# Attention plus MLP on one core: when a slot's copy, its rounding rest, its low weights and its score items are issued

## Chip, cores, metric

One core of one Trainium2 chip. The metric is the device time of one execution in microseconds (us), lower is better; a comparison is made from several rounds in which both kernels run on the same chip. The engines are TensorE (PE, with its weight loads shown as PEld), VectorE (DVE), ScalarE (ACT), GpSimd (POOL) and SyncE (SP, which here only issues transfers). Each engine works through its own instructions in the order in which they were issued, and waits for the others through semaphores.

## What is computed

`x` has 2048 rows of 448 values. It is normalised (layer norm), and three things are added: `x` itself, an attention with 16 heads of 28 and one shared key/value head, and an MLP that normalises once more.

```python
xn = _layernorm(x)
q = (xn @ wq).reshape(B, S, 16, 28);  k = xn @ wk;  v = xn @ wv
p = softmax(einsum("bhqd,bkd->bhqk", q, k) * 28 ** -0.5)
attention = einsum("bhqk,bkd->bhqd", p, v).reshape(B, S, 448) @ wo
y = _layernorm(xn)
mlp = gelu(y @ w1 + b1, approximate=True) @ w2 + b2
out = x + attention + mlp            # w1: 448 x 1792, w2: 1792 x 448
```

## The kernel before, in words

Large products are made from rounded operands: a value is split into a high part in the type fp32r (a copy, "hh", "xh", "w2h") and a rest (value minus high part, rounded: "hl", "xl", "w2l"), and high*high, low*high and high*low are summed in PSUM.

There are three stages. First (to about 66 us) x is normalised and projected to q, k and v, and w1 is split. Second (to about 500 us) the MLP runs, with score work of the attention mixed in. Third the attention proper. The change touches the second stage.

The MLP stage is a row of slots, `slot(n)` at line 631. Slot n belongs to a chunk c of 512 rows and a block ft of 128 of the 1792 hidden columns; there are 4 x 14 = 56 of them, and two more that only drain. A slot holds:

- `mlp1` (line 583): 11 matmuls of 512 columns into the PSUM tile `ph` (one buffer). Then ACT makes `hx` (bias, L590) and `hz` (square, L591), and POOL two steps on `hz` (L592, L593). It hands back two functions for later: `middle` (L596 tanh on ACT, L597 and L598 on POOL) and `ending` (L603, the copy `hh` on ACT, and L605, the rounding rest `hl` on POOL).
- `mlp2` (line 609) for slot n - 2: 12 matmuls of 448 columns with `hh`, `hl` and the rows of w2. After the i-th of them it calls `stages[i]`. The table `stages` is made in `slot` (lines 643 to 646), and a second form of it stands for slots in `norms`.
- In chunk 0 every second slot (`split`, line 580) also splits two blocks of w2: `w2_split` (line 334) has ACT copy the high part (L337) and POOL make the low part (L338); then the next load of w2 is issued (`w2_load`).
- Five slots in each of chunks 0 to 2 (n = 5, 7, 9, 11, 13, then 19 to 27 and 33 to 41 in steps of two) run a step of the next chunk's normalisation, `norms[n]`: PE transposes into the same `ph` buffer, L271 on ACT, L272 on DVE, and the scaling of the next rows (L261 ACT, L262 DVE).

Between these matmuls a slot issues nine score items, spread evenly over its 23 matmuls (lines 681 to 689): the items stand behind matmuls 1, 4, 7, 9, 12, 14, 17, 19 and 22. An item is one matmul of 512 columns into a PSUM tile `m` of a pool with three buffers, and a DVE instruction that empties it. There are two kinds:

- A maximum item (`max_stream`, L508 and L509).
- A turned item (`turned_scores`, L542 and L543). Four of them fill one tile `raw` of 128 x 2048 values; `raw` has two buffers (`RAWS = 2`). After the fourth, two exponentials are queued. `turned_exp` (line 555, L560 on ACT) takes one from the queue each time that it is called; after the second, SP issues four stores of `raw` to DRAM (`td`, L563). The first L543 that writes the buffer again waits for these four stores.

In a slot that is not a `split` slot the first four items are turned items; all others are maximum items. `turned_exp` stands in `stages` twice, as `texp`.

Of the kernel before, what the change touches and what calls it, by code (L numbers as in the profile page):

```python
# [22 lines left out]
NF = F // P  # L23
# [15 lines left out]
def block_kernel(ctx, tc, x, wq, wk, wv, wo, w1, b1, w2, b2, out):  # L39
    nc = tc.nc  # L40
    pe, act, dve, pool = nc.tensor, nc.scalar, nc.vector, nc.gpsimd
    ctx.enter_context(tc.manual_schedule())

    def f(t):
        return t.bitcast(F32)
# [68 lines left out]
    def rawtile(shape):  # L114
        return tmp.tile(shape, F32, name="raw", bufs=2)
# [57 lines left out]
    def proj_steps(ps, wh, wl, xh, xl, cs=slice(0, CW)):  # L173
        n = 0
        ps = ps[:, cs]
        for b in range(3):
            for w, v in ((wh(b), xh[:, b, cs]), (wh(b), xl[:, b, cs]), (wl(b), xh[:, b, cs])):
                pe.matmul(ps, w, v, start=(n == 0), stop=False)  # L178
                n += 1
                yield  # L180
        pe.matmul(ps, wh(3), xh[:, 3, cs], start=False, stop=False)
        yield
        pe.matmul(ps, wh(3), xl[:, 3, cs], start=False, stop=True)
        yield
# [58 lines left out]
    def line(t):  # L243
        lines[t] = keep.tile([P, D], F32, name="a", bufs=4)
        nc.sync.dma_start(lines[t], xv[:, t, :])
# [83 lines left out]
    def w2_load(s):  # L329
        raw = rawtile([P, 2, D])  # L330
        nc.sync.dma_start(raw, w2[2 * s * P:(2 * s + 2) * P, :].rearrange("(b p) n -> p b n", p=P))
        wl_q.append(raw)

    def w2_split(s):
        raw = wl_q.pop(0)
        ab = slice(2 * s, 2 * s + 2)
        act.activation(w2h[:, ab, :], raw, AF.Copy)  # L337
        pool.tensor_sub(w2l[:, ab, :], raw, f(w2h[:, ab, :]))  # L338

    def q_slot(c, i):  # L340
        xh, xl = xts[c, False]
# [91 lines left out]
    for c in range(NCH):  # L433
        center, turn = norm_parts((c + 1) % NCH, c + 1 == NCH)
        for i in range(4):
# [7 lines left out]
            if i in ((2, 3) if c == 0 else (1, 3)):  # L443
                n = 2 * c + i // 3
# [21 lines left out]
    def load_q(u, blocks=range(4)):  # L466
        c, g = units[u]
        cols = slice(c * CW, (c + 1) * CW)
        if u < 2 and 0 in blocks:
            qst.append(xt_p.tile([P, 4, CW], F32R, name="xh"))  # L470
            pool.memset(f(qst[u]), 0.0)
        qs = qst[u % 2]
        for b in blocks:
            blk, i = ((1, 0), (2, 0), (0, 1), (3, 1))[b]
            nh = heads_of(u)
            src = qd[i][4 * DH * g:4 * DH * g + DH * nh, cols].rearrange("(j r) n -> r j n", r=DH)
            loads.dma_start(f(qs[32 * blk:32 * blk + DH, 0:nh, :]), src)
        qss[u] = qs
# [5 lines left out]
    def load_max(u):  # L484
        qs, mr = qss[u], mrs.pop(u)
        nh = heads_of(u)
        pm = mtile([nh * CT, P])
        pe.transpose(pm, mr[:, 0:nh * CT], ident)
        mn = keep.tile([4 * CT, 2, P], F32R, name="mn", bufs=1)[0:nh * CT]
        if u:  # L490
            act.activation(mn[:, 0, :], pm, AF.Copy, scale=-1.0)
        else:
            dve.tensor_scalar(mn[:, 0, :], pm, -1.0, 0.0, op0=ALU.mult, op1=ALU.add)
        dve.scalar_tensor_tensor(mn[:, 1, :], pm, -1.0, f(mn[:, 0, :]), op0=ALU.mult, op1=ALU.subtract)
        loads.dma_start(f(qs[60:61, 0:nh, :]), f(mn[:, 0, :]))
        loads.dma_start(f(qs[124:125, 0:nh, :]), f(mn[:, 1, :]))
# [78 lines left out]
    w2h = hp.tile([P, NF, D], F32R, name="w2h", bufs=1)  # L575
    w2l = hp.tile([P, NF, D], F32R, name="w2l", bufs=1)
# [3 lines left out]
    def split(c, ft):  # L580
        return c == 0 and ft % 2 == 1

    def mlp1(c, ft):
        yh, yl = xts[c, True]
        ph = php.tile([P, CW], F32, name="ph")
        fs = slice(ft * P, (ft + 1) * P)
        yield from proj_steps(ph, lambda b: w1h[:, b, fs], lambda b: w1l[:, b, fs], yh, yl)
        hx = hrp.tile([P, CW], F32, name="hx", bufs=2)
        hz = hrp.tile([P, CW], F32, name="hz", bufs=2)
        act.activation(hx, ph, AF.Identity, bias=b1t[:, ft:ft + 1])  # L590
        act.activation(hz, ph, AF.Square, bias=b1s[:, ft:ft + 1], scale=GELU[0] ** 0.5)  # L591
        pool.tensor_scalar(hz, hz, 1.0, 1.0, op0=ALU.mult, op1=ALU.add)  # L592
        pool.tensor_mul(hz, hz, hx)  # L593

        def middle():
            act.activation(hz, hz, AF.Tanh, scale=GELU[1])  # L596
            pool.tensor_scalar(hz, hz, 0.5, 0.5, op0=ALU.mult, op1=ALU.add)  # L597
            pool.tensor_mul(hx, hx, hz)  # L598

        def ending():  # L600
            hh = hrp.tile([P, CW], F32R, name="hh")
            hl = hrp.tile([P, CW], F32R, name="hl")
            act.activation(hh, hx, AF.Copy)  # L603
            hs[c, ft] = (hh, hl)
            pool.tensor_sub(hl, hx, f(hh))  # L605

        return middle, ending

    def mlp2(c, ft, stages):
        if ft == 0:  # L610
            m2s[c] = [m2p.tile([P, D], F32, name=f"m2_{k}") for k in range(CT)]
        m2 = m2s[c]
        hh, hl = hs.pop((c, ft))
        for k in range(CT):
            ts = slice(k * P, (k + 1) * P)
            pe.matmul(m2[k], hh[:, ts], w2h[:, ft, :], start=(ft == 0), stop=False)  # L616
            stages[3 * k]()
            yield
            pe.matmul(m2[k], hh[:, ts], w2l[:, ft, :], start=False, stop=False)  # L619
            stages[3 * k + 1]()  # L620
            yield
            pe.matmul(m2[k], hl[:, ts], w2h[:, ft, :], start=False, stop=(ft == NF - 1))  # L622
            if ft == NF - 1:
                t = CT * c + k
                a = lines.pop(t)
                dve.tensor_add(a, a, m2[k])
                nc.sync.dma_start(ad[:, t, :], a)
            stages[3 * k + 2]()
            yield

    def slot(n):
        nonlocal maxed
        if n < len(mslots) and split(*mslots[n]):
            blk = n // 2
            w2_split(blk)
            if blk + 2 < NF // 2:
                w2_load(blk + 2)
        middle = ending = none
        if n < len(mslots):
            middle, ending = yield from mlp1(*mslots[n])  # L640
        for _ in range(5 if n < 2 else 0):
            maxed += mxs.step()
        texp = turned_exp if n < len(mslots) - 1 else none
        stages = {1: texp, 2: texp, 5: middle, 9: ending}
        if n in norms:
            stages = {4: norms[n], 5: middle, 6: texp, 7: texp, 10: ending}
        if n >= 2:
            yield from mlp2(*mslots[n - 2], [stages.get(i, none) for i in range(12)])
        else:
            for i in sorted(stages):  # L650
                stages[i]()
# [1 line left out]
    def none():  # L653
        pass

    norms, maxed = {}, 0
    mslots = [(c, ft) for c in range(NCH) for ft in range(NF)]
    for c in range(1, NCH):
        g = norm_gen(c, lambda shape: php.tile(shape, F32, name="ph"))
# [4 lines left out]
    for n in range(len(mslots) + 2):  # L664
        c, ft = mslots[n] if n < len(mslots) else (NCH, n - len(mslots))
        if 3 <= ft < 11 and ft % 2 and c < NCH - 1:
            line(CT * (c + 1) + (ft - 3) // 2)
        if 9 < ft:
            line(CT * c + ft - 10)
            if ft > 10:  # L670
                a = lines[CT * c + ft - 11]
                pool.tensor_add(a, a, b2b)
        if ft == 0 and n:
            a = lines[CT * c - 1]
            pool.tensor_add(a, a, b2b)
        if (c, ft) == (NCH - 1, 8):
            load_q(0)
        if (c, ft) == (NCH - 1, 11):
            load_max(0)
        ts = 0  # L680
        for _ in slot(n):
            done += 1
            if n == len(mslots):
                maxed += mxs.step()
            elif n < len(mslots) and done * MLP_MAX // 46 > (done - 1) * MLP_MAX // 46:
                if ts < 4 and n < len(mslots) - 1 and not split(c, ft):
                    ts += tq.step()
                else:
                    maxed += mxs.step()
# [263 lines left out]
```

## Time and profile before

| what | value |
|---|---|
| median of 3 runs (lowest to highest) | 1139.19 us (1136.71 to 1139.23) |
| the profiled execution: its time | 1138.7 us |
| the profiled execution: its span, first to last instruction | 1136.9 us |
| granted TensorE clock over the span | 0.995 |

In the lists of the profile a row of the timeline gives the start in us, the duration in us, the engine, the line of the kernel, the operation, what it writes and reads, how many instructions are merged in the row, and in brackets the idle time of the engine just before and what ended it. A row of windows gives for each engine the busy time and the number of instructions, then the granted clock, the share of the DMA engines that was busy, and GB/s. "SPq" is SP issuing transfers. The tiles `ph` of the MLP show as `ph`, the w2 accumulators as `m<-w2h,hh` and the score items as `m<-ks,qm` (maximum) and `m<-ks,q` (turned).

### The profile page before, as it was taken

The numbers are of one execution on the slowest core, as the hardware profiler recorded it, in microseconds if no ns is written. First come the engines' busy times: TensorE is split into PE (matmuls) and PEld (weight loads), VectorE is DVE, ScalarE is ACT, GpSimd is POOL, SyncE is SP. The second block draws the span as 40 slices with busy tenths as digits, with TensorE's granted clock in tenths as the row PEclk, the third lists the DMA queues.
The fourth block names the chain that finished last, engine by engine and source line by source line (L and its number), as shares of the span: only waits on it lengthen the run. The fifth ranks groups of instructions, "written<-read, shape, count | busy, mean of one in ns | idle before, by whom it ended". The sixth has DMA issues, their size and how long they took to land.

```text
span 1136.9 us, 17010 instructions
## 1 busy us (share of the span) xinstructions
PE 1103.0 (97%) x5777; PEld 718.4 (63%) x5777; DVE 909.4 (80%) x1704; ACT 723.6 (64%) x953; POOL 564.4 (50%) x690
## 2 busy tenths in 40 slices
PE   9999899999999999999999999999999999999998
PEld 8777787877888888864544555554546444455444
DVE  7787787978888898895888887788886888866733
ACT  6765555666666666656766666467765666664673
POOL 6357787767776777772243425324432342342130
PEclk9999999999999999999999999999999999999999
DMA  8774445767776676866577797587786877975830
GB/s 273 207 226 128 123 109 129 189 172 188 195 191 169 172 204 167 206 179 152 135 176 162 175 230 197 123 206 190 161 195 164 188 169 186 225 162 124 198 85 33
DMA packets 113667, 195.11 MB, mean 172 GB/s; under 512 B 17070, under 2 KB 96100, under 8 KB 109740
## 3 DMA queue, kind: packets, MB, share of 16 engines
q1 hardware_dynamic: 100972, 172.34, 60.7%
q0 software_dynamic: 11200, 21.10, 7.4%
q8 instruction: 46, 0.75, 0.3%
q10 hardware_dynamic: 1408, 0.57, 0.2%
q14 instruction: 41, 0.34, 0.1%
HBM read 115.22 MB, written 77.71 MB: 170 GB/s over the span
## 4 chain that ended last, share of the span: by engine, by line
PE 71%; DVE 7%; DMA 6%; POOL 6%; ACT 5%; issue 2%; SPq 1%; ACTq 0%; DVEq 0%; POOLq 0%
PE po L820 19%; PE m L508 13%; PE s L867 12%; PE ph L178 6%; DVE mx L509 4%; PE m L542 4%; PE m L846 3%; PE m L622 2%; PE m L619 2%; PE m L616 2%; DMA td<-raw 2%; DMA qm<-qd 2%; POOL hx L598 1%; POOL hz L593 1%; PE qp L178 1%
## 5 line engine op out<-in xcount | busy, mean ns | idle before, releaser
L509 DVE TENSOR_REDUCE mx<-m 128x1 f32<-128x512 f32 x784 | 510.7, 685 | 97.1 <-PE m L508 85.9
L869 ACT ACTIVATE p<-s 128x1024 f32<-128x1024 f32 x326 | 315.6, 1027 | 163.0 <-PE s L867 161.6
L508 PE MATMUL m<-ks,qm 128*128 128x512 f32 x784 | 303.2, 411 | 3.0 <-DMA qm<-qd 1.9
L820 PE MATMUL po<-p,vs 128*32 128x512 f32 x2048 | 233.0, 595 | 0.0
L867 PE MATMUL s<-xh,ks 128*128 128x512 f32 x652 | 213.0, 412 | 2.7 <-ACT p L869 0.9
L508 PEld LDWEIGHTS m<-ks,qm 128*128 128x128 f32 x784 | 147.2, 189 | 89.7 <-DVE p L834 45.3
L543 DVE TENSOR_SCALAR_CACHE_REDUCE raw<-m 128x512 f32<-128x512 f32 x240 | 160.5, 689 | 31.6 <-PE m L542 12.9
L867 PEld LDWEIGHTS s<-xh,ks 128*128 128x128 f32 x652 | 114.2, 189 | 57.5 <-ACT p L869 37.2
L820 PEld LDWEIGHTS po<-p,vs 128*32 128x32 f32 x2048 | 60.0, 109 | 133.5 <-issue 132.9
L834 DVE STREAM_TRANSPOSE p<-half 128x1024 f32<-128x1024 f32 x120 | 141.6, 1218 | 3.1 <-PE po L820 3.1
L560 ACT ACTIVATE raw<-raw,m 128x1024 f32<-128x1024 f32 x120 | 133.2, 1151 | 0.0
L542 PE MATMUL m<-ks,q 128*128 128x512 f32 x240 | 97.1, 405 | 5.8 <-DVE raw L543 4.4
L603 ACT ACTIVATE hh<-hx 128x512 fp32r<-128x512 f32 x56 | 35.4, 632 | 97.5 <-POOL hx L598 97.1
L847 ACT ACTIVATE p<-m 128x512 f32<-128x512 f32 x132 | 79.0, 607 | 27.6 <-PE m L846 27.5
L605 POOL TENSOR_TENSOR hl<-hx,hh 128x512 fp32r<-128x512 f32 x56 | 72.4, 1293 | 41.6 <-ACT hh L603 41.6
L622 PE MATMUL m<-w2h,hl 128*128 128x448 f32 x224 | 83.6, 373 | 0.1
L619 PE MATMUL m<-w2l,hh 128*128 128x448 f32 x224 | 82.3, 367 | 0.0
L616 PE MATMUL m<-w2h,hh 128*128 128x448 f32 x224 | 82.0, 366 | 0.0
L593 POOL TENSOR_TENSOR hz<-hz,hx 128x512 f32<-128x512 f32 x56 | 72.5, 1296 | 4.7
L598 POOL TENSOR_TENSOR hx<-hx,hz 128x512 f32<-128x512 f32 x56 | 72.2, 1290 | 4.7
L768 POOL DMA_DIRECT2D tr<-ld x56 | 28.1, 508 | 87.6 <-DMA ld<-rc 87.6
L426 POOL DMA_DIRECT2D qm<-qd x108 | 55.2, 519 | 29.9 <-PE m L508 25.9
(167 smaller groups left out, 1504.8 us busy)
## 6 DMA issues: line engine op xcount, KB each, us to landing
td<-raw SPq DMA_DIRECT2D x240, 256.0 KB
half<-td SPq DMA_DIRECT2D x120, 512.0 KB
xh<-qd POOLq DMA_DIRECT2D x60, 168.0 KB, 7.6
a<-in_A_x_dram SPq DMA_DIRECT2D x32, 224.0 KB
qd<-qe SPq DMA_DIRECT2D x24, 256.0 KB
qm<-qd POOLq DMA_DIRECT2D x108, 56.0 KB, 6.8
qm<-qd SPq DMA_DIRECT2D x88, 56.0 KB
ad<-a SPq DMA_DIRECT2D x16, 224.0 KB
```

What stands on the lines that cost most here:

```text
L508: pe.matmul(pm, qm[:, t * P:(t + 1) * P], ks[:, n * CW:(n + 1) * CW], start=True, stop=True)
L509: dve.tensor_reduce(mx[:, CT * j + t, n:n + 1], pm, axis=AX.X, op=ALU.max)
L542: pe.matmul(sc, q3[i][:, t * P:(t + 1) * P], ks[:, n * CW:(n + 1) * CW], start=True, stop=True)
L543: dve.tensor_scalar(raw[:, :, 4 * n:4 * n + 4, :].rearrange("p r b i -> p b r i"), sc.rearrange("p (b r i) -> p b r i", r=4, i=32), SCALE, ...
L560: act.activation(raw[:, rs], raw[:, rs], AF.Exp, bias=m3[:, 4:5], scale=1.0)
L616: pe.matmul(m2[k], hh[:, ts], w2h[:, ft, :], start=(ft == 0), stop=False)
L619: pe.matmul(m2[k], hh[:, ts], w2l[:, ft, :], start=False, stop=False)
L622: pe.matmul(m2[k], hl[:, ts], w2h[:, ft, :], start=False, stop=(ft == NF - 1))
L820: pe.matmul(po[32 * j:32 * j + 32, :], vs[:, kt, :], ps.pop((u, kt, j)), start=(kt == 0), stop=(kt == NT - 1))
L834: dve.transpose(p.rearrange("p k (g j) -> p g k j", j=32), halves[u, kt // 8][:, :, 32 * (kt % 8):32 * (kt % 8) + 64].rearrange("p g (k j) ...
L867: pe.matmul(s[:, i], ks[:, (kt + k) * P:(kt + k + 1) * P], qss[u][:, j, :], start=True, stop=True)
L869: act.activation(p, s, AF.Exp, scale=SCALE)
```

## The change

Four things are done, all in the MLP stage.

1. `ending` (the copy `hh` on ACT and the rest `hl` on POOL) of slot n is no longer called in slot n but in slot n + 1, at `stages[0]`, where it stands behind that slot's L590 to L593 on ACT and POOL.
2. The low part of w2 is made by DVE, in a function `low` that is called at stage 2 (stage 3 in a `norms` slot); the next load of w2 is issued behind it.
3. The other entries of `stages` move: `texp` from 1 and 2 to 1 and 3; in a `norms` slot the normalisation from 4 to 5, `texp` from 6 and 7 to 6 and 8, `middle` from 5 to 7.
4. The turned items of a slot are its fifth to eighth item, not its first four. The call that queues their exponentials thereby stands behind the slot's last `texp`.

```diff
@@ w2_split
         act.activation(w2h[:, ab, :], raw, AF.Copy)
-        pool.tensor_sub(w2l[:, ab, :], raw, f(w2h[:, ab, :]))
+
+        def low():
+            dve.tensor_sub(w2l[:, ab, :], raw, f(w2h[:, ab, :]))
+            if s + 2 < NF // 2:
+                w2_load(s + 2)
+
+        return low
@@ slot
-        nonlocal maxed
-        if n < len(mslots) and split(*mslots[n]):
-            blk = n // 2
-            w2_split(blk)
-            if blk + 2 < NF // 2:
-                w2_load(blk + 2)
-        middle = ending = none
+        nonlocal maxed, ending
+        middle = low = none
+        closing, ending = ending, none
         if n < len(mslots):
+            if split(*mslots[n]):
+                low = w2_split(n // 2)
             middle, ending = yield from mlp1(*mslots[n])
...
-        stages = {1: texp, 2: texp, 5: middle, 9: ending}
+        stages = {0: closing, 1: texp, 2: low, 3: texp, 5: middle}
         if n in norms:
-            stages = {4: norms[n], 5: middle, 6: texp, 7: texp, 10: ending}
+            stages = {0: closing, 3: low, 5: norms[n], 6: texp, 7: middle, 8: texp}
...
-    norms, maxed = {}, 0
+    norms, maxed, ending = {}, 0, none
@@ the loop over slots
-        ts = 0
+        ts = items = 0
         for _ in slot(n):
...
-                if ts < 4 and n < len(mslots) - 1 and not split(c, ft):
+                items += 1
+                if items > 4 and ts < 4 and n < len(mslots) - 1 and not split(c, ft):
                     ts += tq.step()
                 else:
                     maxed += mxs.step()
```

Slot 0 has only four items, so its four turned items become maximum items, and four turned items move from the MLP stage to the attention stage (which issues what is left of both kinds).

## The prediction

> **What bounds the kernel now.** I read the page first, then windows by chunk, then the timeline of undisturbed slots, then the rows around the longest idle times of PE.
>
> ```profile
> span 1136.9 us, 17010 instructions
> PE 1103.0 (97%) x5777; PEld 718.4 (63%) x5777; DVE 909.4 (80%) x1704; ACT 723.6 (64%) x953; POOL 564.4 (50%) x690
> ```
>
> PE is busy for 97% of the span, so the change can win only where PE waits in the MLP stage, or lose by making it wait. How much there is to win shows in two windows, from L590 of slot 2 to L590 of slot 16 (slots 2 to 15: the rest of chunk 0 and two more), and from there to L590 of slot 55 (39 slots):
>
> ```profile
> core 0: us, PE busy (x) PEld busy (x) DVE busy (x) ACT busy (x) POOL busy (x), PEclk, DMA share, GB/s
> 85.47:197.84 112.37, 103.58 (x453) 84.99 (x452) 88.72 (x174) 60.71 (x87) 87.94 (x80) 0.97 0.47 121
> 197.84:488.50 290.66, 285.08 (x1287) 236.20 (x1286) 250.02 (x577) 189.41 (x252) 212.13 (x206) 1.00 0.72 186
> ```
>
> The yardstick is an undisturbed slot, here on ACT and on POOL:
>
> ```profile
> 415.59 0.69 ACT L590 ACTIVATE hx<-ph,b1t 128x512 f32<-128x512 f32 x1 [0.28 <-PE ph L183]
> 416.17 0.68 ACT L591 ACTIVATE hz<-ph,b1s 128x512 f32<-128x512 f32 x1
> 416.74 2.19 ACT L560 ACTIVATE raw<-raw,m 128x1024 f32<-128x1024 f32 x2
> 422.62 0.69 ACT L590 ACTIVATE hx<-ph,b1t 128x512 f32<-128x512 f32 x1 [0.28 <-PE ph L183]
> ```
> ```profile
> 416.94 0.62 POOL L592 TENSOR_SCALAR hz<-hz 128x512 f32<-128x512 f32 x1 [0.25 <-ACT hz L591]
> ...
> 422.42 1.30 POOL L605 TENSOR_TENSOR hl<-hx,hh 128x512 fp32r<-128x512 f32 x1 [0.74 <-ACT hh L603]
> ```
>
> A slot takes 422.62 - 415.59 = 7.03 us. POOL's chain in it, from L592 to the end of L605, takes 423.72 - 416.94 = 6.78 us: it just fits. Slots with a normalisation need more:
>
> ```profile
> L270 PE MATMUL ph<-ident,xn 128*128 128x128 f32 x48 | 8.3, 299 | 6.0 <-ACT hz L591 6.0
> ```
>
> These are 12 slots with four transposes each, 8.3 / 12 = 0.69 us a slot; four of them lie in the first window, eight in the second. So the first window is 112.37 - 14 x 7.03 - 4 x 0.69 = 11.2 us above undisturbed, the second 290.66 - 39 x 7.03 - 8 x 0.69 = 11.0 us.
>
> **Copy, rest and low part (edits 1 to 3).** In chunk 0 POOL also makes the low part of w2:
>
> ```profile
> 124.67 2.08 POOL L338 TENSOR_TENSOR w2l<-raw,w2h 128x896 fp32r<-128x896 f32 x1
> ```
>
> Every second slot has one, so POOL's chain there needs 6.78 + 2.08 / 2 = 7.82 us a slot against 7.03, and `ph`, which has one buffer, is emptied late. Taking L338 away, and filling POOL's waits by calling L605 a slot later behind L593, cuts the chain to its bare work, well below 7.03. `hl` is needed only by `mlp2` two slots on; issued behind L593 of the next slot it ends some 3.5 us behind that slot's L591, over 2 us before the slot after reaches the matmul that reads it. So the 11.2 us can go. What is paid for it is the low part on DVE:
>
> ```profile
> L803 DVE TENSOR_TENSOR otl<-oc,oth x2: 426/426/427, 1129.1 to 1131.6; 128x256 fp32r<-128x256 f32 x2
> L272 DVE TENSOR_TENSOR xl<-ph,xh x12: 691/692/692, 127.2 to 387.9; 128x512 fp32r<-128x512 f32 x12
> ```
>
> From 0.426 us for 256 columns and 0.692 for 512 follow 1.09 for 896 (estimate); bounds are 0.692 and POOL's 2.08 for the same work. Six of them in the first window raise DVE from 88.72 to 95.3 us, below the 101.2 that the window would then last, so DVE isn't the bound. But `low` stands in DVE's queue in front of L272, on which the next slot's first matmul waits through `ph`, and in front of score items that free `m`. I take 2 us for that (bounds 0, and 6 for twice the duration). Net for chunk 0: -9.2 us.
>
> **The turned items (edit 4).** This is the part that decides. `raw` has two buffers; a buffer filled in slot n is filled again in slot n + 2 and must be stored by then. Before, all fits:
>
> ```profile
> 412.62 0.69 DVE L543 TENSOR_SCALAR_CACHE_REDUCE raw<-m 128x512 f32<-128x512 f32 x1
> ...
> 426.70 0.69 DVE L543 TENSOR_SCALAR_CACHE_REDUCE raw<-m 128x512 f32<-128x512 f32 x1
> ```
>
> The buffer filled from 412.62 is exponentiated by 416.74 + 2.19 = 418.93 and written again at 426.70, 7.77 us later. What the stores need shows where DVE did wait for them; the exponentials of that buffer, SP's issue of four stores in another slot, and DVE's end of the wait:
>
> ```profile
> 343.73 2.18 ACT L560 ACTIVATE raw<-raw,m 128x1024 f32<-128x1024 f32 x2
> ```
> ```profile
> 418.96 3.25 SPq L563 DMA_DIRECT2D td<-raw  x4
> ```
> ```profile
> 352.70 0.69 DVE L543 TENSOR_SCALAR_CACHE_REDUCE raw<-m 128x512 f32<-128x512 f32 x1 [1.08 <-DMA td<-raw]
> ```
>
> From 345.91 to 352.70 are 6.79 us, of which the issue alone is 3.25. So 7.77 left a slack of 1 us.
>
> After the change the fourth turned item of a slot stands behind its 19th matmul, and the last `texp` of that slot behind the 15th: in the changed program's order on ACT each pair of exponentials stands in the next slot, behind `hh`. Counted from L590 of that slot (h): the exponentials ended at h + 3.34 before (418.93 - 415.59); `hh` in front of them adds 0.63 less the 0.1 by which neighbours on ACT overlap (L590 starts 0.58 ahead of L591 and lasts 0.69), so they end at h + 3.87, and the stores land at h + 10.66. The buffer is wanted again by the fifth item of the slot after. That item's place is seen before too:
>
> ```profile
> 133.24 0.40 PE L508 MATMUL m<-ks,qm 128*128 128x512 f32 x1
> ```
> ```profile
> 133.30 0.69 ACT L590 ACTIVATE hx<-ph,b1t 128x512 f32<-128x512 f32 x1 [1.20 <-PE ph L183]
> ```
> ```profile
> 121.60 0.40 PE L508 MATMUL m<-ks,qm 128*128 128x512 f32 x1
> ```
> ```profile
> 122.04 1.33 DVE L509 TENSOR_REDUCE mx<-m 128x1 f32<-128x512 f32 x2 [0.20 <-PE m L508]
> ```
>
> Its matmul starts 0.06 us before L590, and DVE begins 0.44 after a matmul's start: h + 7.03 + 0.38 = h + 7.41. The stores are 3.25 us late, in every slot from 16 on (in chunk 0 only every second slot has turned items, so a buffer rests twice as long there). Behind DVE's waiting L543 stand all score items; `m` has three buffers, so PE stops at the eighth item. The restart:
>
> ```profile
> 464.27 0.69 DVE L543 TENSOR_SCALAR_CACHE_REDUCE raw<-m 128x512 f32<-128x512 f32 x1 [2.46 <-DMA td<-raw]
> ```
> ```profile
> 465.03 0.50 PE L542 MATMUL m<-ks,q 128*128 128x512 f32 x1 [0.98 <-DVE raw L543]
> ...
> 417.65 0.40 PE L508 MATMUL m<-ks,qm 128*128 128x512 f32 x1
> ```
>
> PE goes on 0.76 us after DVE, and from the eighth item (417.65) to the next L590 (422.62) are 4.97, with 0.1 for the slow first matmul 5.07. So L590 of slot n + 2 can't come before that of slot n plus 3.87 + 6.79 + 0.76 + 5.07 = 16.49 us: two slots take 16.49, not 14.06. Loss 2.43 a pair.
>
> In a normalisation slot the exponentials come later:
>
> ```profile
> 354.63 0.69 ACT L590 ACTIVATE hx<-ph,b1t 128x512 f32<-128x512 f32 x1 [0.27 <-PE ph L183]
> ...
> 356.65 0.60 ACT L271 ACTIVATE xh<-ph 128x512 fp32r<-128x512 f32 x1 [0.75 <-PE ph L270]
> ...
> 358.55 2.18 ACT L560 ACTIVATE raw<-raw,m 128x1024 f32<-128x1024 f32 x2
> ```
>
> They end at h + 6.10. `hh` fills the 0.75 in front of L271, and L596 stands among them as before, so I keep 6.10: 6.10 + 6.79 + 0.76 + 5.07 = 18.72 against 14.06 + 0.69. Loss 3.97 a pair; the last of each five does no L261 and loses some 0.7 less. Slots 16 to 54 are 39, of which ten pairs hold a normalisation: 9.5 x 2.43 + 8 x 3.97 + 2 x 3.3 = 61.5 us.
>
> On top comes the clock. PE's start at the eighth item is late by 3.25 + 0.38 + 0.76 - 2.06 = 2.3 us in a plain pair (417.65 is h + 2.06), idle 2.2 since a matmul's 0.40 overlaps the next; in a normalisation pair, where two L590 lie 7.03 + 0.69 = 7.72 apart, by 6.10 + 6.79 - 7.72 + 0.76 - 2.06 = 3.9. What such gaps did:
>
> ```profile
> 125.41 0.48 PE L270 MATMUL ph<-ident,xn 128*128 128x128 f32 x1 [2.37 <-ACT hz L591]
> ...
> 175.50 0.33 PE L270 MATMUL ph<-ident,xn 128*128 128x128 f32 x1 [2.57 <-ACT hz L591]
> ...
> 531.63 0.76 PE L508 MATMUL m<-ks,qm 128*128 128x512 f32 x1 [1.87 <-DMA qm<-qd]
> ...
> 248.85 0.50 PE L542 MATMUL m<-ks,q 128*128 128x512 f32 x1 [1.25 <-DVE raw L543]
> ```
> ```profile
> 125.40:128.80 3.40, 3.39 (x11) 3.03 (x12) 1.60 (x3) 1.31 (x3) 3.22 (x3) 0.50 0.62 172
> 176.60:180.00 3.40, 3.40 (x10) 2.91 (x10) 2.58 (x4) 0.27 (x2) 3.21 (x3) 0.50 0.24 68
> 531.60:535.00 3.40, 3.37 (x8) 2.72 (x9) 1.98 (x3) 1.50 (x3) 0.09 (x1) 0.50 0.03 5
> 248.80:252.20 3.40, 3.35 (x17) 2.72 (x18) 3.18 (x9) 1.54 (x3) 1.51 (x3) 1.00 0.95 234
> ```
>
> All three of 1.87 us and more were followed by 3.4 us at a granted clock of 0.50; the one of 1.25 was not. Half a clock for 3.4 us costs 1.7, and as it falls on the tail of the slot and the first matmuls of the next, it lies on the loop. I take it in all 19.5 pairs, 33.2 us (bounds 0 and 33.2). The Trainium skill (page "TensorE: Matmul & The Clock Gate", Part 1, "What's actually happening") says otherwise: the clock falls to half only after at least one idle window of about 3.4 us. By that rule the plain pairs would keep the clock (second rival); the three gaps above disagree with it.
>
> The four turned items that move to the attention stage cost nothing there: DVE's two kinds last the same, and their two exponentials fall on ACT, which PE covers.
>
> Sum: 1136.9 - 9.2 - 11.0 (the old disturbances of slots 16 to 54, which the loop replaces) + 61.5 + 33.2 = 1211.4 of span. The profiled execution took 1138.7, 1.8 more than its span, and the median is 1139.2: 1213 us.
>
> **Rivals.**
> - The clock falls only in the long stalls, of 3.9 us: 10 x 1.7 in place of 33.2, 1197 us. For it: the rows hold only three cases near 2.2. The skill's page named above would give this.
> - It never falls, since the two slots of a pair share the wait (1.2 each, like the gap of 1.25): 1180 us. Against it: the first wait falls whole into one slot, and nothing evens it out.
> - Not slower: the stores land in time. The point from which it decides is 7.41 - 3.87 = 3.54 us after the exponentials. Then only edits 1 to 3 count: 1136.9 - 9.2 - 11.0 + 1.8 = 1118 us. For it: where DVE didn't wait, the landing isn't seen. Against it: SP needs 3.25 us to issue the four, which leaves the last 0.3.
> - SP is held up by other loads, as for the buffer written again at 464.27, whose exponentials ended at 454.10:
>
> ```profile
> 451.91 2.19 ACT L560 ACTIVATE raw<-raw,m 128x1024 f32<-128x1024 f32 x2
> ```
>
> That took 10.17 us, 3.4 more than 6.79; in four of the pairs, 1226 us.
>
> **From these to the numbers.** Forecast 0.5, long stalls only 0.2, no fall 0.18, SP held up 0.06, not slower 0.06 (nearly all of it faster). 0.3% is about what a measurement of this kernel tells from no change, and no case but the last comes near. Range 1176 to 1228: it reaches from the case without a fall to SP held up, and leaves out the last and the blur of the bounds. Faster 0.05, same 0.01, slower 0.94.
>
> **What would show it.** DVE's idle time in front of L543 ended by the stores of `raw` is the largest wait of the MLP stage, some 80 us (9.5 x 3.25 + 10 x 4.8). Before:
>
> ```profile
> DVE raw L543 <- DMA td<-raw: 12.4, 10, 2.5
> ```
>
> L590 of slots 2 to 16 spans about 103 us, of slots 16 to 55 about 374, with long and short slots in turn and stretches at a clock of 0.50. POOL's wait of L605 for L603 is gone. If DVE hardly waits for the stores, my edit 4 is wrong; if it waits but slots 16 to 55 take about 341, the clock is; if slots 2 to 16 don't get shorter, POOL wasn't the bound of chunk 0.

## The result, and the profile after

| | median of the runs | ratio to before, 95% interval |
|---|---|---|
| before | 1139.21 us (1136.71 to 1141.84) | |
| after | 1210.18 us (1205.29 to 1216.39) | 1.0626 (1.0585 to 1.0668) |

The change makes the kernel 6.3% slower; 1213 us were forecast. The profiled execution of the changed kernel is its shortest, 1205.29 us. In the changed kernel every line from L338 on has a higher number: L590 (`hx`) is now L596, L543 (turned item) L549, L560 (exponentials) L566, L563 (stores) L569, L605 (rest) L611, and DVE's low part is L340.

The head of the page of the profile:

```profile
span 1203.5 us, 17023 instructions
...
PE 1117.9 (93%) x5777; PEld 725.2 (60%) x5777; DVE 917.2 (76%) x1711; ACT 713.8 (59%) x953; POOL 550.8 (46%) x683
```

PE works 15 us longer than before (slots 16 to 54 hold ten stretches of 3.41 us at half clock), the span is 66.6 us longer, and so PE's share falls from 97% to 93%. The same two windows as before, from L596 of slot 2 to that of slot 16, and on to that of slot 55 (columns: PE, PEld, DVE, ACT, POOL busy, granted clock, DMA share, GB/s):

```profile
83.74:188.99 105.25, 101.98 (x466) 84.91 (x465) 98.09 (x187) 57.99 (x84) 79.21 (x75) 1.00 0.46 122
188.99:550.28 361.29, 303.51 (x1283) 245.18 (x1282) 249.14 (x578) 180.78 (x250) 209.65 (x207) 0.95 0.60 150
```

Before, they took 112.37 and 290.66. So the 66.6 us of span are: -1.7 ahead of slot 2 (85.47 to 83.74), -7.1 in slots 2 to 15, +70.6 in slots 16 to 54, and +4.8 behind (the rest of the span is 653.2, it was 648.4). The stretch of +70.6 seen closer, over two slots without a normalisation (rows of the timeline, most left out):

```profile
481.93 0.69 ACT L596 ACTIVATE hx<-ph,b1t 128x512 f32<-128x512 f32 x1 [5.00 <-PE ph L183]
...
483.60 2.19 ACT L566 ACTIVATE raw<-raw,m 128x1024 f32<-128x1024 f32 x2
...
485.81 3.25 SPq L569 DMA_DIRECT2D td<-raw  x4
...
489.02 0.69 ACT L596 ACTIVATE hx<-ph,b1t 128x512 f32<-128x512 f32 x1 [2.71 <-PE ph L183]
...
492.68 0.69 DVE L549 TENSOR_SCALAR_CACHE_REDUCE raw<-m 128x512 f32<-128x512 f32 x1 [3.48 <-DMA td<-raw]
...
493.44 0.50 PE L548 MATMUL m<-ks,q 128*128 128x512 f32 x1 [2.19 <-DVE raw L549]
...
498.53 0.69 ACT L596 ACTIVATE hx<-ph,b1t 128x512 f32<-128x512 f32 x1 [5.13 <-PE ph L183]
```

The reader sees the predicted chain. The exponentials end at 485.79, which is h + 3.86 (483.60 + 2.19 - 481.93). SP issues four stores at once. 6.89 us after the exponentials DVE may write the buffer, at 492.68, after an idle time of 3.48; PE goes on 0.76 later, having stood for 2.19. The slots take 7.09 and 9.51 us in turn, 16.60 a pair; forecast were 16.49. The waits of the changed kernel:

```profile
DVE raw L549 <- DMA td<-raw: 55.6, 20, 5.3
...
PE m L548 <- DVE raw L549: 50.3, 25, 4.0
```

The wait for the stores is 55.6 us (it was 12.4). POOL's wait of L605 for L603, 41.6 us before, is in the list no more.

### The profile page after: what moved, and what is told of

The parts are those of the page before. It is cut to its first block, busy times and chain, and to the rows that moved or that the text cites. A ratio compares the mean times of both kernels' runs of the same rounds, so it can differ in the third digit from the quotient of the medians.

```text
span 1203.5 us, 17023 instructions
## 1 busy us (share of the span) xinstructions
PE 1117.9 (93%) x5777; PEld 725.2 (60%) x5777; DVE 917.2 (76%) x1711; ACT 713.8 (59%) x953; POOL 550.8 (46%) x683
## 4 chain that ended last, share of the span: by engine, by line
PE 66%; DMA 11%; DVE 9%; ACT 7%; SPq 3%; issue 3%; POOL 1%; ACTq 0%; DVEq 0%; POOLq 0%
PE po L825 18%; PE m L514 13%; PE s L872 11%; DMA td<-raw 7%; PE ph L178 6%; DVE mx L515 4%; ACT raw L566 3%; PE m L548 3%; PE m L851 3%; DMA qm<-qd 3%; SPq L569 2%; PE m L628 2%; PE m L622 2%; PE m L625 2%; PE m L736 1%
## 5 line engine op out<-in xcount | busy, mean ns | idle before, releaser
L514 PE MATMUL m<-ks,qm 128*128 128x512 f32 x784 | 311.1, 419 | 17.6 <-DVE raw L549 7.1
L549 DVE TENSOR_SCALAR_CACHE_REDUCE raw<-m 128x512 f32<-128x512 f32 x240 | 156.5, 688 | 91.4 <-DMA td<-raw 55.6
L514 PEld LDWEIGHTS m<-ks,qm 128*128 128x128 f32 x784 | 150.1, 192 | 117.6 <-DVE p L839 45.3
L596 ACT ACTIVATE hx<-ph,b1t 128x512 f32<-128x512 f32 x56 | 38.6, 690 | 217.6 <-PE ph L183 215.2
L548 PE MATMUL m<-ks,q 128*128 128x512 f32 x240 | 100.9, 420 | 50.7 <-DVE raw L549 50.3
L566 ACT ACTIVATE raw<-raw,m 128x1024 f32<-128x1024 f32 x120 | 134.8, 1151 | 0.0
L598 POOL TENSOR_SCALAR hz<-hz 128x512 f32<-128x512 f32 x56 | 35.2, 628 | 173.0 <-ACT hz L597 172.9
L548 PEld LDWEIGHTS m<-ks,q 128*128 128x128 f32 x240 | 45.4, 189 | 71.6 <-DVE raw L549 60.5
L599 POOL TENSOR_TENSOR hz<-hz,hx 128x512 f32<-128x512 f32 x56 | 75.5, 1348 | 4.7
```

What stands on the lines that cost most here:

```text
L514: pe.matmul(pm, qm[:, t * P:(t + 1) * P], ks[:, n * CW:(n + 1) * CW], start=True, stop=True)
L548: pe.matmul(sc, q3[i][:, t * P:(t + 1) * P], ks[:, n * CW:(n + 1) * CW], start=True, stop=True)
L549: dve.tensor_scalar(raw[:, :, 4 * n:4 * n + 4, :].rearrange("p r b i -> p b r i"), sc.rearrange("p (b r i) -> p b r i", r=4, i=32), SCALE, ...
L566: act.activation(raw[:, rs], raw[:, rs], AF.Exp, bias=m3[:, 4:5], scale=1.0)
```

## Experiments

In the expectations, theory A is the prediction's: the two buffers of `raw` are filled again before their stores have landed. B says that the loss comes from the copy and rest that are issued late, or from the low part in DVE's queue. C says that DVE's L262 (the scaling of 64 columns in a normalisation), which is held up while POOL works, is behind it. All ratios are to the kernel before.

### Edits 1 to 3 without edit 4

```diff
-                if items > 4 and ts < 4 and n < len(mslots) - 1 and not split(c, ft):
+                if ts < 4 and n < len(mslots) - 1 and not split(c, ft):
```

> Edits 1 to 3 alone: the turned items are a slot's first four again, so their exponentials run in the same slot. Theory A (the two buffers of raw: refilled before their stores land): the wait for the stores falls back to some 12 us or less, and what is left is the shorter POOL chain: L590 of slots 2 to 16 spans about 105 us as in the changed kernel, of slots 16 to 55 about 285 to 292; time 1128 us (1120 to 1136). The exponentials end 0.53 us later than before (behind the copy), which leaves 0.45 of the 1 us of slack. Theory B (the loss comes from the copy and the rest being late, or from the low part in DVE's queue, which backs up the three buffers of m): still about 1200 us.

Measured: 1130.31 us (1127.48 to 1133.72), ratio 0.9929 (0.9907 to 0.995). Its windows by slots 2, 16 and 55:

```profile
84.28:188.96 104.68, 101.82 (x466) 85.07 (x465) 98.13 (x186) 59.56 (x86) 79.22 (x75) 1.00 0.51 133
188.96:476.93 287.97, 280.64 (x1283) 236.29 (x1282) 255.96 (x577) 180.88 (x250) 210.26 (x207) 1.00 0.74 187
```

The gain in chunk 0 is all there (104.68), and slots 16 to 54 are as quick as before. The whole loss hangs on edit 4.

### Edit 4 alone

The kernel before, with the turned items as a slot's fifth to eighth item:

```diff
-                if ts < 4 and n < len(mslots) - 1 and not split(c, ft):
+                items += 1
+                if items > 4 and ts < 4 and n < len(mslots) - 1 and not split(c, ft):
```

> The kernel before with edit 4 alone: only the turned items move to places five to eight. Theory A: the exponentials run in the next slot and end at h + 3.34 (no copy in front of them), so the stores are 2.72 us late and a plain pair of slots takes 15.96 us, a normalisation pair as long as in the changed kernel; with half of the pairs losing 1.7 us to the clock, 1195 us (1180 to 1212), and chunk 0 is as long as before (112 us). Theory B: 1139 us, within 10.

Measured: 1220.7 us (1218.88 to 1222.26), ratio 1.0721 (1.0699 to 1.0743): slower still than the changed kernel. B is refuted, since copy, rest and low part are where they were. A has the direction, but the time lies above its range (1180 to 1212). The second window, and the wait:

```profile
197.20:566.73 369.53, 306.40 (x1280) 248.91 (x1279) 243.42 (x577) 189.55 (x251) 212.95 (x208) 0.94 0.58 148
```
```profile
DVE raw L543 <- DMA td<-raw: 78.1, 21, 6.2
```

Slots 16 to 54 take 369.5, which is 89.8 above an undisturbed 279.7 (39 x 7.03 + 8 x 0.69). The clock fell 13 times in them, 22 us at 1.7 each, and slot 55 to the end takes 653.3 in place of 648.4, for which the expectation had nothing. The rest of the miss stays open.

### The exponentials in their own slot

The changed kernel, with `texp` behind the slot's eighth item:

```diff
-        stages = {0: closing, 1: texp, 2: low, 3: texp, 5: middle}
+        stages = {0: closing, 2: low, 5: middle, 8: texp, 10: texp}
...
-            stages = {0: closing, 3: low, 5: norms[n], 6: texp, 7: middle, 8: texp}
+            stages = {0: closing, 3: low, 5: norms[n], 7: middle, 8: texp, 10: texp}
```

> The changed kernel, with both exponentials called at stages 8 and 10 of their own slot, behind the call that queues them; the turned items stay the fifth to eighth. Theory A: the exponentials end at about h + 6.3, the stores land at h + 13.1, and the buffer is wanted at h + 14.44: no wait, no fall of the clock, 1120 us (1112 to 1130). If instead late turned items are bad in themselves (theory B, or less room on DVE in the second half of a slot): about 1200 us as in the changed kernel.

Measured: 1130.9 us (1126.43 to 1134.63), ratio 0.993 (0.9904 to 0.9956). The items stay as edit 4 puts them; only the exponentials, and so the stores, start earlier. The wait for the stores is gone:

```profile
DVE raw L549 <- DMA td<-raw: 0.8, 1, 0.8
```

That takes 79 us off edit 4's price: the loss is the time from the last turned item of a fill to the landing of its stores, not the place of the items. But the run is some 10 us over the expected 1120, just outside its range. In slots 16 to 54 most slots without a normalisation take 7.03 us, the longest 7.63; six with one take 8.85 to 8.90. One of these (unfiltered timeline):

```profile
227.80 1.34 DVE L262 TENSOR_SCALAR xn<-a,lnq,lnqb 128x64 f32<-128x64 f32 x1
227.81 1.29 POOL L611 TENSOR_TENSOR hl<-hx,hh 128x512 fp32r<-128x512 f32 x1
...
229.06 0.68 DVE L549 TENSOR_SCALAR_CACHE_REDUCE raw<-m 128x512 f32<-128x512 f32 x1
...
229.81 0.50 PE L514 MATMUL m<-ks,qm 128*128 128x512 f32 x1 [1.13 <-DVE raw L549]
```

L262 works on 64 columns and lasts 1.34 us, until POOL's L611 ends; behind it the turned items are late, and PE stands for 1.13. The same line in the kernel before and in the changed one, all its runs in the MLP stage (min/median/max in ns):

```profile
L262 DVE TENSOR_SCALAR xn<-a,lnq,lnqb x12: 304/352/948, 107.7 to 372.9; 128x64 f32<-128x64 f32 x12
```
```profile
L262 DVE TENSOR_SCALAR xn<-a,lnq,lnqb x12: 657/1311/1382, 107.7 to 412.9; 128x64 f32<-128x64 f32 x12
```

Moving L611 into the next slot (edit 1) put it beside L262. This was not foreseen.

### The low part back on POOL

Edits 1 and 3, with the low part on POOL; it stays at edit 2's later place in the slot, and so does the next load of w2:

```diff
-            dve.tensor_sub(w2l[:, ab, :], raw, f(w2h[:, ab, :]))
+            pool.tensor_sub(w2l[:, ab, :], raw, f(w2h[:, ab, :]))
```

> Edit 1 with its spacing of the stages, but the low part of w2 back on POOL (called at stage 2 or 3) and the turned items first. Theory A: POOL's bare work is 5.1 us a slot, with half of 2.08 on top 6.2, below 7.03, so chunk 0 is as short as with the low part on DVE (105 us for slots 2 to 16): 1126 us (1118 to 1136). Rival: it was the low part on DVE that relieved chunk 0, and without it slots 2 to 16 span 112 us again: 1137 us.

Measured: 1128.83 us (1127.1 to 1131.01), ratio 0.9917 (0.9899 to 0.9935), the first window 105.60. So chunk 0 is relieved without DVE: beside edit 1, by which POOL no longer waits for `hh` (a wait of 41.6 us before), the move of the low part to DVE adds 0.9 us in this window and nothing in the time. That L605's later call does it, and not the low part's later place on POOL, is argued: no run has edit 1 with the low part at its old place.

### The stores on two queues

The changed kernel, with two of the four stores issued by ACT:

```diff
-                nc.sync.dma_start(td[u][:, :, 4 * t + a, :],
+                (nc.scalar if a % 2 else nc.sync).dma_start(td[u][:, :, 4 * t + a, :],
```

> The changed kernel with two of the four stores of raw issued by ACT, two by SP; nothing else. Theory A (the loop through raw's stores sets the pace): the issue of four takes SP 3.25 us, of two 1.6, so the stores land some 1.6 us earlier; a plain pair loses 0.8 us in place of 2.43, a normalisation pair some 2.4 in place of 3.97, and only the latter can still lose the clock: L590 of slots 16 to 55 spans 310 to 325 us (361 in the changed kernel), time 1150 to 1180 us. If the landing hangs on the transfer and not on the issue, or the loop isn't the cause: 1205 us or more.

Measured: 1218.25 us (1211.32 to 1223.77), ratio 1.0691 (1.0655 to 1.0728): not A's 1150 to 1180; the expectation's other branch came, 1205 or more "if the landing hangs on the transfer and not on the issue". One fill in the timeline, and the window of its transfer:

```profile
201.55 2.19 ACT L566 ACTIVATE raw<-raw,m 128x1024 f32<-128x1024 f32 x2
...
203.76 1.21 SPq L569 DMA_DIRECT2D td<-raw  x2
203.77 1.85 ACTq L569 DMA_DIRECT2D td<-raw  x2
...
210.34 0.69 DVE L549 TENSOR_SCALAR_CACHE_REDUCE raw<-m 128x512 f32<-128x512 f32 x1 [3.25 <-DMA td<-raw]
```
```profile
204.80:209.90 5.10, 4.33 (x20) 3.38 (x18) 2.06 (x3) 3.38 (x5) 3.35 (x4) 1.00 0.86 206
```
The same in the changed kernel, for the fill ahead of the one shown first:

```profile
474.23 2.18 ACT L566 ACTIVATE raw<-raw,m 128x1024 f32<-128x1024 f32 x2
...
483.18 0.69 DVE L549 TENSOR_SCALAR_CACHE_REDUCE raw<-m 128x512 f32<-128x512 f32 x1 [1.07 <-DMA td<-raw]
```
```profile
477.60:482.70 5.10, 5.10 (x24) 4.31 (x23) 4.35 (x10) 0.77 (x2) 1.41 (x2) 1.00 0.86 206
```

All four are issued within 1.9 us and not 3.25, yet DVE goes on 6.60 us after the exponentials (210.34 - 203.74); in the changed kernel it was 6.77 (483.18 - 476.41). In both kernels the 1 MB moves in about 5.1 us at 206 GB/s with the DMA engines busy for 0.86. Over all fills of slots 15 to 53 for which DVE stood more than 0.5 us, the time from the exponentials' end to DVE's start is 6.77 to 9.27 with a median of 7.0 in the changed kernel, and 6.60 to 9.72 with a median of 7.1 with two queues. So issuing faster did not make the stores land earlier; that the transfer sets the landing is read from these windows. This kernel is even 8 us slower than the changed one: slots 16 to 54 take 365.9 us (361.3), with half-clock stretches of 41.0 us in all (34.1), and the part behind slot 55 takes 657.7 (653.2). Why the latter is longer stays open.

### Edit 2 alone, at two places

The kernel before, with the low part on DVE. In the first run it stands where POOL's stood, at the start of the slot:

```diff
-        pool.tensor_sub(w2l[:, ab, :], raw, f(w2h[:, ab, :]))
+        dve.tensor_sub(w2l[:, ab, :], raw, f(w2h[:, ab, :]))
```

> The kernel before with edit 2 alone: the low part of w2 on DVE, at its old place at the slot's start. POOL's chain falls from 7.82 to 6.78 us a slot in chunk 0, just below 7.03. If POOL's load is what bounds chunk 0: slots 2 to 16 span about 106 us (112 before), 1132 us (1127 to 1137). If it is the place of the copy and the rest in the queues that counts, 111 us or more and 1138.

Measured: 1163.38 us (1162.39 to 1165.86), ratio 1.0214 (1.02 to 1.0229): neither number of the expectation. The first window takes 134.3 us in place of 112.4, and the timeline shows why:

```profile
94.12 0.63 ACT L603 ACTIVATE hh<-hx 128x512 fp32r<-128x512 f32 x1 [2.11 <-POOL hx L598]
94.66 0.93 ACT L337 ACTIVATE w2h<-raw 128x896 fp32r<-128x896 f32 x1
...
95.62 1.42 DVE L338 TENSOR_TENSOR w2l<-raw,w2h 128x896 fp32r<-128x896 f32 x1 [3.59 <-ACT w2h L337]
96.97 3.07 DVE L509 TENSOR_REDUCE mx<-m 128x1 f32<-128x512 f32 x5
...
97.70 0.50 PE L508 MATMUL m<-ks,qm 128*128 128x512 f32 x1 [3.44 <-DVE mx L509]
```

ACT makes `hh` first, which waits for POOL, then the high part of w2; DVE's low part waits for that, and all score items of the slot wait behind it on DVE. If this is the cause, the same work at a later place costs nothing, which the second run tries (the next load of w2 behind it, as in the change):

```diff
-        stages = {1: texp, 2: texp, 5: middle, 9: ending}
+        stages = {1: texp, 2: texp, 3: low, 5: middle, 9: ending}
```

> The kernel before, and the low part of w2 on DVE as in the run at 1163, but issued behind the third step of mlp2 (stage 3), with the next load of w2 behind it; copy and rest stay where they were before. If the loss of that run came from the place in DVE's queue (low at the head of the slot, waiting for ACT's high part, which stands behind the copy hh and so behind POOL, with all score items of the slot behind it), this one loses none of it: ACT's high part is long done when DVE comes to low, PE's waits of 3.4 us for L509 are gone, slots 2 to 16 take 104 to 109 us and the kernel 1128 to 1134. If it came from the work of 1.1 to 1.4 us on DVE itself, it stays near 1160.

Measured: 1133.93 us (1131.75 to 1135.37), ratio 0.9956 (0.9939 to 0.9972), the first window 106.51. The place was worth 29 us, the work itself hides (the next load of w2 moved with it, but in neither run does ACT's copy of w2 wait for a load):

```profile
94.83 1.20 DVE L340 TENSOR_TENSOR w2l<-raw,w2h 128x896 fp32r<-128x896 f32 x1
```

It starts without a wait. So edit 2 does relieve chunk 0 (112.4 to 106.5) where edit 1 isn't there; either suffices. That both remove the same excess on POOL fits, but is argued.

### L262 on ACT

In the kernel of edits 1 and 3:

```diff
-            dve.tensor_scalar(xn[:, D:512], src[:, 384:448], scale[:, t:t + 1], bias[:, t:t + 1],
-                              op0=ALU.mult, op1=ALU.add)
+            if second and c:
+                act.activation(xn[:, D:512], src[:, 384:448], AF.Identity, bias=bias[:, t:t + 1], scale=scale[:, t:t + 1])
+            else:
+                dve.tensor_scalar(xn[:, D:512], src[:, 384:448], scale[:, t:t + 1], bias[:, t:t + 1],
+                                  op0=ALU.mult, op1=ALU.add)
```

> The fourth kernel of the first four (edit 1 with its spacing, low part on POOL, turned items first), and the 64 columns of L262 are scaled by ACT in the MLP stage, not by DVE. Theory C: in a normalisation slot DVE's L262 lasts 1.35 us in place of 0.30 since it waits for POOL's instruction (the rest is issued there now), and PE loses 1.1 us at the next slot's start; without it slots 16 to 55 span about 281 us in place of 288 and slots 2 to 16 some 2 less: 1120 us (1115 to 1125). If the 1.1 us come from the wait for ACT's L271 instead: 1129 us.

Measured: 1119.24 us (1117.2 to 1121.26), ratio 0.9825 (0.9809 to 0.9842). On ACT the step lasts 0.43 us, and nothing waits for it. The first window takes 101.79, against 101.2 undisturbed.

The same edit with the turned items at 5 to 8 and the exponentials in their own slot (low part on POOL):

> As the one before, but with turned items as the fifth to eighth and both exponentials at stages 8 and 10 of their own slot. Theory A and C together: no wait for the stores in any slot, 280 us for slots 16 to 55, within 3 us of the one before (1117 to 1123). If late turned items had a cost of their own, it shows here as more than 3 us.

Measured: 1118.63 us (1115.58 to 1127.35), ratio 0.9835 (0.9807 to 0.9863). These two are the quickest found, and can't be told apart. Windows of the second:

```profile
82.45:185.58 103.13, 101.80 (x466) 84.81 (x465) 88.95 (x177) 61.49 (x91) 90.11 (x83) 1.00 0.51 133
185.58:466.15 280.57, 280.11 (x1283) 236.00 (x1282) 246.22 (x570) 188.69 (x258) 210.27 (x207) 1.00 0.75 191
```

Slots 16 to 54 take 280.6, with 279.7 undisturbed: edit 4 itself costs nothing once its stores start early enough and L262 is off DVE.

The same edit in the changed kernel as it is:

> The changed kernel, and the 64 columns of L262 scaled by ACT instead of DVE in the normalisations of chunks 1 to 3. In the kernels with edits 1 and 3 that step alone was worth about 9.6 us (1128.8 to 1119.2), where the next slot stood 1.13 us on DVE. A: in the changed kernel the two buffers of raw set the loop, and a normalisation slot of that kernel gains only where DVE's turned items, not the stores, end last: between 3 us (the four normalisation slots of chunk 0) and 10 us less than its 1210, so 1200 to 1207, with the wait for the stores still over 50 us. C: if the conflict of L262 with POOL were the main cause of the loss and the wait for the stores its consequence, 1150 or less.

Measured: 1205.53 us (1202.99 to 1209.04), ratio 1.0589 (1.0568 to 1.061). C is refuted as the cause of the loss. The second window, and the wait:

```profile
186.97:554.65 367.68, 306.74 (x1283) 249.82 (x1282) 241.68 (x570) 183.61 (x259) 210.04 (x207) 0.94 0.58 147
```
```profile
DVE raw L552 <- DMA td<-raw: 84.4, 24, 5.8
```

With L262 out of the way the same loop stands on the stores all the more, 84.4 us.

## Why the prediction was right, point by point

**What bounds, and which edit decides.** Right: undoing edit 4 takes 80 us away, edit 4 alone brings 82 (1220.7 - 1139), and starting the stores earlier removes all of it (1130.9 against 1130.31).

**Chunk 0.** A gain of 9.2 was forecast; 1.7 + 7.1 = 8.8 came. But the 2 us that I charged for the low part in DVE's queue were charged to the wrong instruction. Low part on DVE or on POOL makes the first window 104.68 or 105.60; taking L262 off DVE takes it from 105.60 to 101.79. The duration of 1.09 us was right only where no POOL instruction was under way when L340 began (1.08, once in these rows of the changed kernel, min/median/max in ns); the other six began while one was, and lasted longer:

```profile
L340 DVE TENSOR_TENSOR w2l<-raw,w2h x7: 1081/1284/2177, 79.8 to 168.0; 128x896 fp32r<-128x896 f32 x7
```

**The loop through `raw`.** Slots 16 to 54 take 361.3 us, 81.6 above undisturbed. The clock fell ten times in them; at the prediction's 1.7 us each that is 17.0, and 64.6 remain for the loop. 61.5 were forecast. Its links agree one by one: exponentials at h + 3.86 (3.87), landing 6.89 later (6.79; over all fills the median is 7.0), PE 0.76 behind DVE, a plain pair of 16.60 (16.49). A normalisation pair agrees too: from L596 of slot 37 (389.27) to that of slot 39 (409.63) are 20.36 us, with one fall of the clock in it, so 18.7 without (18.72). Only its exponentials come sooner than forecast, at h + 5.03 to 5.91 in the ten normalisation slots, not 6.10. The wait of 55.6 us is below the "some 80": here other releasers are named for part of DVE's idle time (91.4 us in all ahead of L549), and with L262 gone it is 84.4.

**The clock: the term that was mis-sized.** 33.2 us were forecast, a fall in each of 19.5 pairs; 17.0 came. The profiled span lies 7.9 below the sum (1203.5 against 1211.4: +3.1 loop, -16.2 clock, +0.4 in and ahead of chunk 0, +4.8 attention). The rule I took from three gaps, that 1.87 us of idle time are enough and 1.25 are not, lacks a condition. Three stalls of the changed kernel, by windows of 3.41 us (busy PE is the third number, the granted clock the third from the end):

```profile
339.19:342.60 3.41, 1.47 (x7) 0.96 (x6) 0.43 (x1) 3.41 (x5) 2.72 (x3) 1.00 0.73 199
342.60:346.01 3.41, 3.08 (x8) 2.62 (x9) 2.95 (x10) 0.21 (x1) 2.26 (x3) 0.50 0.70 157
438.18:441.59 3.41, 1.69 (x9) 1.16 (x7) 0.00 (x0) 3.41 (x6) 2.51 (x3) 1.00 0.90 222
441.59:445.00 3.41, 1.93 (x9) 1.69 (x10) 2.65 (x10) 0.43 (x1) 2.49 (x3) 1.00 0.68 161
445.00:448.42 3.42, 3.42 (x17) 2.83 (x16) 3.21 (x6) 0.27 (x1) 0.00 (x0) 1.00 0.81 200
506.45:509.86 3.41, 1.35 (x7) 0.89 (x5) 0.38 (x1) 3.41 (x5) 3.23 (x4) 1.00 0.77 192
509.86:513.27 3.41, 3.04 (x8) 2.58 (x9) 2.97 (x10) 0.10 (x1) 2.14 (x3) 0.50 0.91 215
```
```profile
443.07 0.51 PE L548 MATMUL m<-ks,q 128*128 128x512 f32 x1 [3.20 <-DVE raw L549]
```

All falls of an execution start on one grid of 3.41 us. In the windows ahead of 342.60 and 509.86 PE is idle for 1.94 and 2.06 us, and the clock is halved in the next. The gap of 3.20 us that ends at 443.07 is longer, but it is cut by the grid at 441.59 into 1.72 and 1.48, and the clock stays.

So a gap of 2 to 3 us trips it only where most of it lies in one window. PE stands for 2 us or more sixteen times in slots 16 to 54. Nine of these stalls follow a normalisation slot (2.37 to 3.98 us), and eight of them tripped the clock; seven lie in plain pairs (2.05 to 2.43), and two of them did (342.60 and 509.86). In the other plain pairs, in slots 17 to 20 and 51 to 54, both slots share the wait, as the second rival says, and no stall reaches 1.5 us.

The rule of the Trainium skill that the prediction weighed (page "TensorE: Matmul & The Clock Gate", Part 1, "What's actually happening") names a free-running window of 3413 ns, and here the trace agrees; that it needs a whole idle window the trace denies, since 1.94 us idle of 3.41 did. Of the ten windows ahead of a fall only one was idle throughout (243.61 to 247.02).

The first rival, falls in the ten long stalls only, therefore had the clock term right, 10 x 1.7, though which stalls tripped it was not quite as it says. Its 1197 lies 8 below the profiled execution (1205.29) for the other reasons, the 3.1 of the loop and the 4.8 of the attention above all. That my 1213 comes within 3 us of the median is in part luck: the clock was over-sized by 16, other terms were short by 8, and the executions of the changed kernel run from 1205.29 to 1216.39, with a granted clock from 0.984 down to 0.974. How often the clock falls may thus differ between executions of one kernel.

**The attention stage.** I costed the moved items at nothing there. The part behind slot 55 takes 4.8 us more than before (653.2), and the kernel with the exponentials in their own slot doesn't have it (648.0), though the same items moved. (In the kernels here without the loss this part takes 647.6 to 650.8, so some 2 of the 4.8 us are no more than kernels differ by.) In the changed kernel one fill's exponentials are left over for the attention (unfiltered timeline):

```profile
576.84 1.15 ACT L566 ACTIVATE raw<-raw,m 128x1024 f32<-128x1024 f32 x1
...
578.02 5.61 SPq L569 DMA_DIRECT2D td<-raw  x4
...
595.30 0.77 PE L514 MATMUL m<-ks,qm 128*128 128x512 f32 x1 [4.29 <-DMA qm<-qd]
```

ACT comes to the second half of that fill only at 576.84; its stores move in the midst of the loads that begin the attention, and PE waits 4.29 us for one of these (1.87 before), with a halved clock behind it. That the stores delay this load is read from the order in time; it wasn't tried by itself.

**The rival on the other side** (stores land in time) fell, as the landing of 6.6 us and more against the 3.54 allowed shows. My reason against it, SP's 3.25 us of issue, was not the limit: with the issue halved the landing stayed. The transfer of 5.1 us fits, and it didn't shrink with a second queue. A third buffer of `raw` wasn't tried. The rival with SP held up by other loads didn't come as a rule: eight of the 30 fills took more than 7.5 us from the exponentials to DVE, the longest 9.27.

## What to carry to other kernels

Where a buffer goes round (fill, work, store, fill), write down the time of each link in the slot's own time, and compare the sum with the turns that the buffers allow: here a move of four items by half a slot, with the work behind them a slot later, took 4.2 us (7.77 - 3.54) from a slack of 1. Work that fills a buffer late in a slot needs its next step in the same slot. Before an instruction is placed in an engine's queue, ask what its input waits for on the other engine: the same low part on DVE cost 24 us at the head of the slot and gained some 5 a few matmuls later.

## What the runs showed of the hardware

- The clock's window, above: halved for a stretch of 3.41 us after a window of the grid with PE idle for about 1.8 us or more. By the PE rows of the executions the least idle time in a window ahead of a fall is 1.77 us (edits 1 to 3), and the most without one 1.88 (stores on two queues), so the threshold is known to about that; some matmul records may be missing, and the ends of matmuls are modelled. One fall does not fit: at 74.38 in the kernel with edit 2 alone at stage 3, with 0.99 us idle ahead of it. A halved stretch of 6.83 us occurs too (twice in slots 16 to 54 with two queues).
- DVE's scaling of 64 columns from and to SBUF lasts 0.30 us alone and up to 1.38 beside a POOL instruction; in the changed kernel all twelve in the MLP stage end 0.05 us behind the end of a POOL instruction. The Trainium skill (page "SBUF — State Buffer", "SBUF: two separate sides") has a port pair that DVE and GpSimd share as an exclusive lock, held for the whole instruction by whichever starts first, for DVE instructions in a 2-port mode or with two SBUF inputs. The trace agrees (1.34 against 1.29 for POOL's, begun together); whether L262 runs in such a mode no run here shows. On ACT the same step takes 0.43 whatever POOL does, worth 9.6 us to the kernel with edits 1 and 3.
- Four stores of 256 KB took about 5.1 us of transfer (206 GB/s) in the two windows above, with one queue and with two.
